# A complex-decay attention and expert kernel: the order of the program from a fixed table instead of a planner

## Chip, cores, metric

The kernel runs on 1 core of one Trainium2 chip. The metric is the device time of one execution in microseconds; before the change it is 220.39 us, the median of three runs (220.15 to 220.47).

## What is computed

Four batches, eight heads, 768 time steps, head width 48. Each step scales a 48x48 complex state per head by a decay and adds an outer product; the output row is read with `q` and goes through a layer norm and a two-layer network with 1536 hidden columns.

```python
scale = np.minimum(mag, 0.999) / (mag + 1e-06)        # mag = |a|
for t in range(S):
    new_re = ar * S_re - ai * S_im
    new_im = ar * S_im + ai * S_re
    S_re, S_im = (new_re + kv, new_im)                # kv = outer(k_t, v_t)
    y[:, :, t] = np.einsum('bhd,bhde->bhe', q[:, :, t], S_re)
...
xn = (x - mu) / np.sqrt(var + 1e-06) * g_ln           # x: y with its heads side by side
out = x + np.maximum(xn @ w_ch1, 0.0) @ w_ch2
```

## The kernel before

The 768 steps of a batch are cut into chunks of 128, and two chunks make a pair: 12 pairs `P`, 24 chunks `n`. Lines are those of the profile.

**Decays and phases of a pair.** SP loads `are`, `aim` (128 x 768) and, chunk by chunk, `k`, `q` and `vf` (line 402 to 411). ScalarE takes the logarithm and the inverse of `are` (429, 431), VectorE forms the ratio `r` (423), its square `r2` is made by GpSimd, VectorE or ScalarE, ScalarE takes log(1 + r2) (444), VectorE puts the log magnitude `l` together and clamps it (449, 451). TensorE sums it over time with triangular matrices `u_e` (463, `dec`), ScalarE takes both exponentials `e` and `en` (468). For the phase ScalarE takes the arctangent `th` (472), TensorE sums it (479, 482, `ph`), VectorE keeps the last row as the carry `car` (492) and makes the absolute value `sh` (499, or ScalarE 497), ScalarE takes sine and cosine into `trig` (502, 505). Logarithms and trigonometry need different tables in ScalarE, loaded at line 676, once for a unit of two pairs.

**Attention of a pair.** `ke` and `qe` are `k` and `q` times the exponentials, `ks` and `qs` those times cosine and sine (line 423; `tt` gives all of these one line, told apart by tile). `ks` and `qs` of a chunk are transposed, by TensorE (534) with a copy (384, 382) or by a DMA transpose on SP (542), fixed for each pair by `CROSSBAR`. `am` is the score matrix (558), `atm` its masked copy (423 from `banks` and `mask`), `gm` adds the chunk to the state (571 puts the old state in with an identity product, 575 adds), `G` scales it by the chunk's decay `dec`, `y` is the output (593, 596), `x` its copy. The decays of the two chunks come per unit: TensorE sums `l` (690), ScalarE takes `et` (697), TensorE spreads it (705), VectorE copies `dec` (709).

**Network of a pair.** Norm statistics (606, 607), `rstd` on GpSimd (624, 626), transposes of `x` (614), the copy `xT` (617), the first product (638), `relu` on ScalarE (647), the second product (656), `ot` on VectorE (662), the store (667). The first weights are folded with the norm's weights once, in the head: 27 matmuls (371) and nine copies.

**The order.** Every step is an `Op` with costs; `Graph.order` walks time with guessed costs, keys and slacks per engine, picks for each engine the next step, chooses between alternatives such as GpSimd or VectorE for `ke`, and gives out the eight PSUM banks. Steps marked `lock` are planned so that VectorE and GpSimd don't run them at once. Each engine then executes its instructions in the order so found. The weights `w1b` and `w2b` are loaded by GpSimd (352, 354) behind its constants.

Of the kernel before, what the change touches and what calls it, by code (L numbers as in the profile page):

```python
# [43 lines left out]
BIAS = {"abs": 0.402, "r2": 0.226, "ke": -1.349, "qe": 1.158, "kT": 1.307, "qT": 0.801, "wc": -0.23, "x": 0.392}  # L44
CHUNK = 0.212
SLACK = {"PE": 0, "ACT": 0.051, "DVE": 0.16, "POOL": 0.598, "SP": 0.016}
LATENCY = 0.18
WARM = 22.0


class Op:
# [8 lines left out]
class Graph:  # L60


    def __init__(self, rings, n_banks=8):
        self.ops, self.rings = {}, rings
        self.n_banks = n_banks
        self.bank = {}

    def add(self, name, eng, cost, group, pos, emit, needs=(), uses=(), ps=None, alt=None, tail=0.0, c=0, lock=False):
        assert name not in self.ops, name
        alts = {eng: (cost, tail)}  # L70
        for e, c_ in alt or ():
            alts[e] = (c_, tail)
        self.ops[name] = Op(name, alts, group, pos, emit, list(needs), list(uses), ps)
        self.ops[name].c = c
        self.ops[name].lock = lock

    def order(self, keys):
        ops = self.ops
        for op in ops.values():
            op.key = op.pos + keys[op.group] + (CHUNK * op.c)  # L80
        touch, owner_ops = {}, {}
        for op in ops.values():
            for kind, idx in op.uses:
                touch.setdefault((kind, idx), []).append(op)
            if op.ps:
                owner_ops.setdefault(op.ps[0], []).append(op)
        for op in ops.values():
            preds = {ops[n].name for n in op.needs}
            for kind, idx in op.uses:
                for o in touch.get((kind, idx - self.rings[kind]), ()):  # L90
                    preds.add(o.name)
            preds.discard(op.name)
            op.preds = [ops[n] for n in preds]
            for p in op.preds:
                p.users.append(op)
            op.left = len(op.preds)
        free = {e: 0.0 for e in ("PE", "ACT", "DVE", "POOL", "SP")}
        dma_free = lock_free = 0.0
        bank_free = [0.0] * self.n_banks
        bank_used = [None] * self.n_banks  # L100
        owner_left = {o: len(v) for o, v in owner_ops.items()}
        owner_end = {}
        ready = {e: [] for e in free}
        for op in ops.values():
            if op.left == 0:
                for e in op.alts:
                    ready[e].append(op)
        done, queued = [], []

        def choose(n):  # L110
            best = None
            if n == 2:
                for i in range(0, self.n_banks, 2):
                    if bank_used[i] is None and bank_used[i + 1] is None:
                        t = max(bank_free[i], bank_free[i + 1])
                        if best is None or t < best[0]:
                            best = (t, i)
            else:
                for i in range(self.n_banks):
                    if bank_used[i] is None:  # L120
                        t = (bank_used[i ^ 1] is None, bank_free[i])
                        if best is None or t < best[0]:
                            best = (t, i)
                if best:
                    best = (best[0][1], best[1])
            return best

        total = len(ops)
        while len(done) < total:
            pick = None  # L130
            for e, cands in ready.items():
                ests = []
                for op in cands:
                    t = free[e]
                    for p in op.preds:
                        t = max(t, p.end + (LATENCY if p.eng != e else 0.0))
                    if op.ps and op.ps[0] not in self.bank:
                        b = choose(op.ps[1])
                        if b is None:
                            continue  # L140
                        t = max(t, b[0])
                    if e in ("POOL", "DVE") and op.lock:
                        t = max(t, lock_free)
                    if len(op.alts) > 1:
                        main = next(iter(op.alts))
                        end = t + op.alts[e][0] + (BIAS[op.group] if e != main else 0.0)
                        if any(max(free[x], t if x == "POOL" else 0.0) + op.alts[x][0]
                               + (BIAS[op.group] if x != main else 0.0) < end - 0.01
                               for x in op.alts if x != e):
                            continue  # L150
                    ests.append((t, op))
                if not ests:
                    continue
                t0 = min(x[0] for x in ests) + SLACK[e]
                t, op = min((x for x in ests if x[0] <= t0), key=lambda x: (x[1].key, x[0]))
                if pick is None or t < pick[0]:
                    pick = (t, op, e)
            assert pick is not None, [o.name for v in ready.values() for o in v]
            t, op, e = pick
            cost, tail = op.alts[e]  # L160
            if e == "PE" and t < WARM:
                cost *= 2
            op.eng = e
            if op.ps and op.ps[0] not in self.bank:
                i = choose(op.ps[1])[1]
                self.bank[op.ps[0]] = i
                for j in range(i, i + op.ps[1]):
                    bank_used[j] = op.ps[0]
            free[e] = t + cost
            if e in ("POOL", "DVE") and op.lock:  # L170
                lock_free = t + cost
            op.start, op.cost = t, cost
            op.end = t + cost
            if tail and e == "POOL":
                for o, at in queued:
                    if at > t:
                        o.end += tail
                dma_free = max(dma_free, t + cost) + tail
                op.end = t + cost + tail + 1.8
            elif tail:  # L180
                queued.append((op, max(dma_free, t + cost)))
                dma_free = max(dma_free, t + cost) + tail
                op.end = dma_free + 1.8
            if op.ps:
                o = op.ps[0]
                owner_left[o] -= 1
                owner_end[o] = max(owner_end.get(o, 0.0), op.end)
                if owner_left[o] == 0:
                    i = self.bank[o]
                    for j in range(i, i + op.ps[1]):  # L190
                        bank_used[j] = None
                        bank_free[j] = owner_end[o] + LATENCY
# [13 lines left out]
def kernel(  # L206
# [116 lines left out]
    def c_ident():  # L323
        make_identity(nc, ident)
# [423 lines left out]
```

## Time and profile before

| | before |
|---|---|
| median of 3 runs | 220.39 us (220.15 to 220.47) |
| profiled execution | 218.72 us |
| its span, first to last instruction | 217.0 us |
| TensorE busy | 181.4 us, 1874 matmuls |
| VectorE, ScalarE, GpSimd busy | 167.5, 152.5, 68.6 us |
| moved by DMA | 38.84 MB, 179 GB/s |

The span is what the trace shows; the execution's own time lies 1.7 us above it. Busy time is the union of an engine's instructions. Matmuls overlap in the trace, so what one costs is the distance from its start to the next start and not its duration. An idle engine costs nothing unless the chain that ends last runs through it.

### The profile page before, as it was taken

Reading aid. Unit: us, or ns where it says so; the run is one execution under the profiler, and the core shown is the slowest. Engines: PE = TensorE matmul, PEld = TensorE weight load, DVE = VectorE, ACT = ScalarE, POOL = GpSimd, SP = SyncE. Lnnn points to the kernel's source line nnn. Section 1 sums busy time; section 2 is a strip of 40 time slices with the busy share of each in tenths; the row PEclk is TensorE's granted clock in tenths of the full one; section 3 lists DMA queues with packets and bytes.
Section 4 is the critical chain, followed back from the end, with each engine's and each line's share of the span. In section 5 each row is a group of like instructions: output and inputs, shape, how many; then the busy total and the mean of one; then the engine's idle time right before and its main releaser. Section 6 shows DMA issues by size and latency. Waiting matters only on the chain.

```text
span 217.0 us, 4784 instructions
## 1 busy us (share of the span) xinstructions
PE 181.4 (84%) x1874; PEld 132.7 (61%) x1875; DVE 167.5 (77%) x294; ACT 152.5 (70%) x188; POOL 68.6 (32%) x106
## 2 busy tenths in 40 slices
PE   0027565789899999988999899999999999899993
PEld 0012244347699668776586686677856688677861
DVE  0663288999799998999998897789989899772122
ACT  4545468679799878699486998989997882525410
POOL 8980103055003355303790012920057201301000
PEclk9999999699999999999999999999999999999999
DMA  6999999999999999499999899988983178720212
GB/s 180 310 199 197 193 238 234 217 199 284 194 226 184 242 266 194 84 220 246 234 232 190 188 142 232 244 179 186 201 167 93 37 121 210 101 73 3 73 67 78
DMA packets 137350, 38.84 MB, mean 179 GB/s; under 512 B 132336, under 2 KB 136944, under 8 KB 137328
## 3 DMA queue, kind: packets, MB, share of 16 engines
q1 hardware_dynamic: 135376, 36.19, 77.4%
q0 software_dynamic: 1952, 2.36, 6.3%
q8 instruction: 14, 0.23, 0.4%
q14 instruction: 8, 0.07, 0.1%
HBM read 28.31 MB, written 4.72 MB: 152 GB/s over the span
## 4 chain that ended last, share of the span: by engine, by line
PE 41%; DVE 23%; ACT 23%; DMA 5%; issue 4%; SPq 1%; DVEq 0%; ACTq 0%
PE banks L656 13%; PE banks L638 9%; ACT h L647 4%; PE banks L463 3%; DVE l L449 3%; ACT trig L502 3%; DVE l L451 3%; PE banks L558 3%; ACT trig L505 2%; PE banks L482 2%; ACT are L431 2%; DVE r L423 2%; ACT L676 2%; DVE sh L499 2%; PE banks L371 2%
## 5 line engine op out<-in xcount | busy, mean ns | idle before, releaser
L638 PE MATMUL banks<-xT,w1b 128*128 128x256 bf16 x432 | 52.8, 272 | 0.5 <-ACT h L647 0.3
L656 PE MATMUL banks<-w2b,h 128*128 128x384 bf16 x288 | 52.3, 326 | 0.0
L638 PEld LDWEIGHTS <-w1b 128*128 128x128 bf16 x432 | 40.6, 98 | 6.0 <-issue 1.1
L647 ACT ACTIVATE h<-banks 128x1024 bf16<-128x1024 f32 x36 | 36.4, 1021 | 11.0 <-PE banks L638 10.8
L656 PEld LDWEIGHTS <-h 128*128 128x128 bf16 x288 | 26.9, 98 | 15.1
L423 POOL TENSOR_TENSOR qe<-q,e 128x384 bf16<-128x384 f32 x24 | 23.6, 1003 | 27.5 <-ACT e L468 18.5
L423 DVE TENSOR_TENSOR atm<-banks,mask 128x1024 bf16<-128x1024 f32 x24 | 28.6, 1215 | 1.3 <-PE banks L558 1.1
L662 DVE SCALAR_TENSOR_TENSOR ot<-banks,rstd,x 128x384 f32<-128x384 f32 x24 | 14.7, 611 | 16.6 <-PE banks L656 12.4
L463 PE MATMUL banks<-l,u_e 128*128 128x384 f16 x48 | 11.0, 357 | 16.7 <-DVE l L451 16.7
L624 POOL TENSOR_SCALAR rstd<-mv 128x2 f32<-128x2 f32 x12 | 4.3, 361 | 62.0 <-DVE mv L607 62.0
L468 ACT ACTIVATE e<-banks 128x768 bf16<-128x768 f32 x12 | 9.7, 810 | 14.8 <-PE banks L463 14.3
L463 PEld LDWEIGHTS <-u_e 128*128 128x128 f16 x48 | 4.6, 103 | 21.0 <-issue 15.6
L676 ACT ACT_TABLE_LOAD x12 | 15.4, 1283 | 1.0 <-PEq L732 0.8
L558 PE MATMUL banks<-qsT,ksT 96*128 96x128 bf16 x192 | 14.5, 224 | 0.9 <-DMA ksT<-ks 0.9
L449 DVE SCALAR_TENSOR_TENSOR l<-r,w 128x768 f16<-128x768 f16 x12 | 11.4, 951 | 4.5 <-ACT r L444 4.5
L423 DVE TENSOR_TENSOR r<-aim,are 128x768 f16<-128x768 f32 x12 | 11.8, 985 | 4.0 <-ACT are L431 3.7
L502 ACT ACTIVATE trig<-banks 128x768 bf16<-128x768 int16 x12 | 9.7, 811 | 7.1 <-PE banks L482 4.4
L423 DVE TENSOR_TENSOR qs<-qe,trig 128x768 bf16<-128x768 bf16 x24 | 14.6, 623 | 0.1
L414 POOL TENSOR_SCALAR v<-vf 128x768 bf16<-128x768 f32 x12 | 10.6, 889 | 12.3 <-DMA vf<-in_v_dram 12.3
L505 ACT ACTIVATE trig<-sh,quarter 128x768 bf16<-128x768 f16 x12 | 11.3, 942 | 4.1 <-DVE sh L499 4.0
L423 DVE TENSOR_TENSOR ks<-ke,trig 128x768 bf16<-128x768 bf16 x24 | 13.9, 603 | 0.0
L558 PEld LDWEIGHTS <-ksT 96*128 96x128 bf16 x192 | 12.0, 100 | 3.1 <-DMA ksT<-ks 1.2
(79 smaller groups left out, 354.1 us busy)
## 6 DMA issues: line engine op xcount, KB each, us to landing
are<-in_a_re_dram SPq DMA_DIRECT2D x12, 384.0 KB, 4.8
aim<-in_a_im_dram SPq DMA_DIRECT2D x12, 384.0 KB, 4.9
k<-in_k_dram SPq DMA_DIRECT2D x24, 192.0 KB, 4.0
q<-in_q_dram SPq DMA_DIRECT2D x24, 192.0 KB, 3.8
vf<-in_v_dram SPq DMA_DIRECT2D x24, 192.0 KB, 3.9
out_dram<-ot SPq DMA_DIRECT2D x24, 192.0 KB, 2.2
w1b<-in_moe_w_ch_dram POOLq DMA_DIRECT2D x1, 1152.0 KB, 9.7
w2b<-in_moe_w_ch_dram POOLq DMA_DIRECT2D x1, 1152.0 KB, 17.0
```

Of the source, the lines that this page charges most:

```text
L414: add(("v", P), "POOL", .82, lock=True, emit=lambda: nc.gpsimd.tensor_scalar(out=T("v", P), in0=T("vf", P), scalar1=1.0, scalar2=0.0, op0= ...
L423: engine(name).tensor_tensor(**kw)
L449: nc.vector.scalar_tensor_tensor(out=flat(T("l", P)), in0=flat(T("r2", P)), scalar=0.5, in1=flat(T("w", P)), op0=ALU.mult, op1=ALU.add)
L463: nc.tensor.matmul(heads(ps[:, c, 0:DM]), lhsT=u_e[:, c, j], rhs=step(T("l", P), j), start=(j == 0), stop=(j == R - 1))
L502: add(("sin", P), "ACT", .7, lambda: act(out=T("trig", P)[:, 1], in_=v16(), func=AF.Sin, scale=TWO_PI_SAFE / TURN), needs=[("ph", P)], use ...
L505: add(("cos", P), "ACT", .83, lambda: act(out=T("trig", P)[:, 0], in_=T("sh", P), func=AF.Sin, scale=-TWO_PI_SAFE / TURN, bias=quarter), n ...
L558: nc.tensor.matmul(ps[:, h], lhsT=T("ksT", n)[0:D2, h], rhs=T("qsT", n)[0:D2, h], start=True, stop=True)
L638: nc.tensor.matmul(ps[:, jj], lhsT=w1b[:, dc, ts(gi * JG + jj, C)], rhs=T("xT", P)[:, dc].rearrange("p c t -> p (c t)"), start=(dc == 0), ...
L647: add(("relu", P, gi), "ACT", .91, lambda gi=gi, o=o: act(out=T("h", P)[:, ts(gi, JG)], in_=bank2(o).rearrange("p s (j t) -> p (s j) t", t ...
L656: nc.tensor.matmul(bank(("o", n))[:, 0:DM], lhsT=T("h", P)[:, j, ts(c, C)], rhs=w2b[:, j], start=(j == 0), stop=(j == NJ - 1))
L662: add(("ot", n), "DVE", .54, lambda n=n, c=c: nc.vector.scalar_tensor_tensor(out=T("ot", n), in0=bank(("o", n))[:, 0:DM], scalar=T("rstd", ...
L676: nc.scalar.preload_act_table_set({"log": "natural_log_exp_and_others", "trig": "trig_and_small"}[name])
```

## The change

**Table.** `KEYS`, `BIAS`, `CROSSBAR` and the planner go. `PLAN` is one list of steps for all engines, each with its engine and, where it has one, its first PSUM bank; `Graph.run` asserts the dependences and emits the steps in that order. Which engine does a step, which transposes go over DMA and where the tables are loaded all stand in the list.

**Halves.** `PARTS = {0: 2}`: pair 0 runs its decay and phase steps in two halves of four heads, with one PSUM bank each.

**Decays.** They are taken for a whole pair: 16 one-column matmuls read the last row of `e` (line 547), and `G` is scaled only after a pair's second chunk; after the first it is a plain copy, and the second chunk adds to the same bank without the identity product. The 48 rows of cosine and of sine lie at partitions 0 and 64, so that `ks`, `qs`, their transposes and `G` use all 128.

**Weights.** `w1b` and `w2b` are issued after a one-column probe of a tile that the load of `k` (pair 0, second chunk) or `aim` (pair 1) writes.

**Fill-ins.** `warm` steps are matmuls of 256 columns on constants into a free bank; the table has 52, all ahead of the first transposes.

**Engines.** `r`, `ks` and `qs` may run on GpSimd, `relu` on VectorE, `G`, `xT`, `car` and `dec` on ScalarE; `ot` may be split into a scaling on ScalarE (`oa`) and a sum on GpSimd; `atm` may be masked on GpSimd.

```diff
-CROSSBAR = {"ks": (6, 7, 8, 9, 10, 11), "qs": (3, 4, 5, 6, 7, 8, 9, 10, 11)}
+PARTS = {0: 2}
+GATES = {"gate.0": "k.0.1", "gate.1": "aim.1.0"}
+PLAN = """
+ue:G car0.1:G are.0.0:S pad.ks.0:G car0.0:G tab.log.0:A ln.0.0:A iv.0.0:A ident:G cmat.0:G are.0.1:S one:G
...
-    for op in g.order(KEYS):
-        op.emit()
+    g.run(PLAN)
...
+        g.add(name, lambda: nc.gpsimd.tensor_copy(out=probe, in_=t()[:, 0, 0:1]), needs=[GATES[name]])
...
+                        nc.tensor.matmul(bank(f"dps.{P}")[ds(a * HALF, D), ds(h, 1)],
+                                         lhsT=T("e", P)[96:C, R - 1, ts(h, D)],
+                                         rhs=ident[96:C, C - 1:C], start=True, stop=True)
...
-                    if not nfirst:
-                        nc.tensor.matmul(ps, lhsT=ident[0:D2, 0:D2],
+                    if c == 0 and not nfirst:
+                        nc.tensor.matmul(ps, lhsT=ident,
...
-                                         lhsT=T("ks", P)[:, c, h, 0:D2],
+                        nc.tensor.matmul(heads(ps)[:, h], lhsT=T("ks", P)[:, c, h],
...
+                if c == 0:
+                    add(f"G.{n}", lambda n=n: put(f"G.{n}", T("G", n),
+                                                  heads(bank(f"gm.{P}")[:, 0:DM])),
...
+                if eng(f"relu.{P}.{gi}") == "ACT":
+                    act(out=dst, in_=src, func=AF.Relu)
+                else:
+                    nc.vector.tensor_scalar(out=dst, in0=src, scalar1=0.0, scalar2=None, op0=ALU.max)
...
+            add(f"oa.{n}", lambda n=n, c=c: nc.scalar.mul(
+                out=T("ot", n), in_=bank(f"o.{n}")[:, 0:DM], mul=T("rstd", P)[:, ds(c, 1)]),
...
+                if eng(f"ot.{n}") == "POOL":
+                    nc.gpsimd.tensor_tensor(out=T("ot", n), in0=T("ot", n), in1=T("x", n), op=ALU.add)
...
+        g.add(f"warm.{i}", lambda i=i: nc.tensor.matmul(
+            bank(f"warm.{i}")[:, 0:256], lhsT=u_e[:, 0, 0], rhs=u_e[:, 1].rearrange(
+                "p j t -> p (j t)"), start=True, stop=True), needs=["ue"], ps=(f"warm.{i}", 1))
```

The order is shown at three places (the number behind a name is its buffer). The first is SP at the program's start, before:

```order
L402 DMA are_64<-in_a_re_dram 128x8x96
L402 DMA aim_67<-in_a_im_dram 128x8x96
L402 DMA are_65<-in_a_re_dram 128x8x96
L402 DMA aim_68<-in_a_im_dram 128x8x96
L402 DMA are_66<-in_a_re_dram 128x8x96
L402 DMA aim_69<-in_a_im_dram 128x8x96
L407 DMA k_73<-in_k_dram 128x8x48
L407 DMA q_70<-in_q_dram 128x8x48
```

and now:

```order
L434 DMA are_64<-in_a_re_dram 128x4x96 x2
L434 DMA aim_67<-in_a_im_dram 128x4x96 x2
L434 DMA are_65<-in_a_re_dram 128x8x96
L434 DMA are_66<-in_a_re_dram 128x8x96
L434 DMA aim_68<-in_a_im_dram 128x8x96
L393 DMA k_73<-in_k_dram 128x8x48
L359 DMA gln<-in_moe_g_ln_dram 128x3x1
L393 DMA k_73<-in_k_dram 128x8x48
L393 DMA q_70<-in_q_dram 128x8x48
L434 DMA aim_69<-in_a_im_dram 128x8x96
L393 DMA q_70<-in_q_dram 128x8x48
```

The loads of pair 0 come in half tiles, its second `k` stands ahead of both `q`, and the last of `aim` between them.

The second is GpSimd where it issues the weights, before (the memsets fill the unused columns of `ks` and `qs`):

```order
L339 AFFINE_SELECT cmat<-cmat 128x384 x3
L294 MEMSET ks_112 128x16x32
L294 MEMSET ks_113 128x16x32
L294 MEMSET ks_114 128x16x32
L294 MEMSET qs_115 128x16x32
L294 MEMSET qs_116 128x16x32
L294 MEMSET qs_117 128x16x32
L352 DMA w1b<-in_moe_w_ch_dram 128x3x1536
L354 DMA w2b<-in_moe_w_ch_dram 128x12x384
L423 TENSOR_TENSOR qe_110<-q_70,e_99 128x384 x2
```

and now:

```order
L351 COPY probe<-k_73 128x1
L355 DMA w1b<-in_moe_w_ch_dram 128x3x1536
L345 MEMSET qs_113 128x32x16
...
L351 COPY probe<-aim_68 128x1
L403 TENSOR_SCALAR v_78<-vf_76 128x768
L345 MEMSET qs_114 128x32x16
L277 TENSOR_TENSOR qe_109<-q_71,e_98 128x384 x2
L357 DMA w2b<-in_moe_w_ch_dram 128x12x384
L277 TENSOR_TENSOR ke_107<-k_74,en_100 128x384 x2
```

The two weight loads no longer stand side by side: the second waits behind the `v` of pair 0 and the `qe` of pair 1.

The third is VectorE where the network of pair 0 begins, before:

```order
L423 TENSOR_TENSOR ks_112<-ke_109,trig_103 128x16x48
L423 TENSOR_TENSOR r_85<-aim_68,are_65 128x768
L384 COPY ksT_118<-banks 96x1024
L384 COPY ksT_119<-banks 96x1024
L606 BN_STATS stats_144<-x_134 128x6
L607 BN_AGGR mv_147<-stats_144 128x2
L423 TENSOR_TENSOR atm_127<-banks,mask 128x1024
L423 TENSOR_TENSOR atm_128<-banks,mask 128x1024
L423 TENSOR_TENSOR r_86<-aim_69,are_66 128x768
L449 SCALAR_TENSOR_TENSOR l_90<-r_87,w_82 128x768
L451 TENSOR_SCALAR l_90<-l_90 128x768
L662 SCALAR_TENSOR_TENSOR ot_162<-banks,rstd_152,x_133 128x384
```

and now:

```order
L277 TENSOR_TENSOR ks_111<-ke_107,trig_102 128x16x48 x2
L274 COPY qsT_123<-banks 128x1024
L274 COPY qsT_122<-banks 128x1024
L698 TENSOR_SCALAR h_158<-banks 128x1024
L274 COPY ksT_118<-banks 128x1024
L653 BN_STATS stats_141<-x_131 128x6
L654 BN_AGGR mv_145<-stats_141 128x2
L277 TENSOR_TENSOR qs_115<-qe_108,trig_103 128x16x48 x2
L277 TENSOR_TENSOR atm_126<-banks,mask 128x1024
L277 TENSOR_TENSOR atm_124<-banks,mask 128x1024
L698 TENSOR_SCALAR h_158<-banks 128x1024
```

Two of the pair's three relu (`h`, line 698) stand on VectorE, and the ratios `r` have left it.

## Rows read from the trace of the kernel before

**Rows 1.** The page: busy time, share and instructions of each engine
```profile
PE 181.4 (84%) x1874; PEld 132.7 (61%) x1875; DVE 167.5 (77%) x294; ACT 152.5 (70%) x188; POOL 68.6 (32%) x106
```

**Rows 2.** Stretches: length, busy of PE, PEld, DVE, ACT, POOL, clock, DMA
```profile
25.00:43.20 18.20, 11.14 (x66) 7.13 (x67) 15.45 (x25) 12.11 (x15) 2.63 (x3) 0.91 1.11 227
43.20:190.00 146.80, 139.55 (x1586) 105.91 (x1585) 134.80 (x244) 120.07 (x151) 50.19 (x62) 1.00 0.90 189
190.00:213.50 23.50, 23.48 (x200) 16.69 (x197) 7.33 (x14) 7.11 (x8) 0.92 (x2) 1.00 0.16 57
```

**Rows 3.** Chain that ended last: start us, length us, what
```profile
0.79 3.54 DMA are<-in_a_re_dram
...
11.86 1.45 PE banks L463 x4
...
43.33 0.65 PE banks L463 x4
43.98 0.88 PE banks L371 x4
...
82.92 0.45 PE banks L705 x8
...
201.75 3.93 PE banks L638 x36
205.68 7.82 PE banks L656 x48
```

**Rows 4.** Timeline of TensorE, 50 to 57 us: start us, duration us, what
```profile
50.38 0.18 PE L593 MATMUL banks<-v,atm 128*128 128x48 bf16 x1
50.41 0.18 PE L596 MATMUL banks<-G,qsT 96*128 96x48 bf16 x1
...
54.49 0.33 PE L571 MATMUL banks<-G,ident 96*96 96x384 bf16 x1
54.66 0.50 PE L575 MATMUL banks<-v,ks 128*96 128x48 bf16 x8
55.00 0.61 PE L558 MATMUL banks<-qsT,ksT 96*128 96x128 bf16 x8
55.44 0.33 PE L479 MATMUL banks<-car,pick 96*128 96x384 f16 x1
...
56.43 0.61 PE L534 MATMUL banks<-ident,ks 128*96 128x128 bf16 x8
```

**Rows 5.** Groups by line and shape: busy us, mean ns of one
```profile
L647 ACT ACTIVATE h<-banks 128x1024 bf16<-128x1024 f32 x36 | 36.4, 1021 | 11.0 <-PE banks L638 10.8
L423 DVE TENSOR_TENSOR atm<-banks,mask 128x1024 bf16<-128x1024 f32 x24 | 28.6, 1215 | 1.3 <-PE banks L558 1.1
L676 ACT ACT_TABLE_LOAD x12 | 15.4, 1283 | 1.0 <-PEq L732 0.8
L431 ACT ACTIVATE are<-w 128x768 f32<-128x768 f32 x12 | 10.1, 845 | 0.3
L382 ACT CAST x<-banks 128x384 bf16<-128x384 f32 x18 | 8.4, 479 | 6.9 <-PE banks L596 6.9
```

**Rows 6.** Landing of loads: of `q` before 60 us, and of `w1b`
```profile
DMA to landing us min/median/max: 3.4/3.9/13.4
w1b<-in_moe_w_ch_dram POOLq DMA_DIRECT2D x1, 1152.0 KB, 9.7
```

**Rows 7.** Line 451, `qe`: ns min/median/max; all of 451; GpSimd's timeline at 10 us
```profile
L451 DVE TENSOR_SCALAR l<-l x12: 359/361/1775, 10.0 to 162.2; 128x768 f16<-128x768 f16 x12
L423 POOL TENSOR_TENSOR qe<-q,e x24: 903/914/1616, 14.2 to 166.1; 128x384 bf16<-128x384 f32 x24
L451 DVE TENSOR_SCALAR l<-l 128x768 f16<-128x768 f16 x12 | 8.1, 675 | 0.4
...
10.13 1.46 POOL L294 MEMSET qs<- 128x512 bf16 x3
```

**Rows 8.** Waits of SP's queue: us in total, times, longest
```profile
SPq L667 <- DVE ot L662: 35.5, 11, 6.9
```

More of the change, by code (lines that the diff above doesn't have):

```diff
@@ new lines @@
+relu.0.0:A4 decc.1:A7 r.3.0:G gm.2:P6 qs.2.0.0:V mm1.0.2.1:P0 am.3:P4 iv.4.0:A G.2:A6 r2.3.0:A qs.2.0.1:V
+qT.5:P7 gm.3:P6 atm.2:V2 atm.3:V4 y.2:P2 mm2.1.0:P3 y.3:P4 mm2.0.0:P5 mm2.1.1:P3 relu.0.2:V0 u.3.0:A r.4.0:G
+rstd.0:G l.3.0:V x.2:A2 xtr.2:P2 mm2.0.1:P5 mm2.1.2:P3 x.3:V4 mm2.0.2:P5 k.4.0:S dec.3.0:P0 xtr.3:P4 k.3.1:S
+ke.2.0.1:V r2.4.0:A u.4.0:A tab.trig.1:A th.3.0:A G.3:V6 qsT.5:V7 xT.2:A2 ot.1:V3 xT.3:V4 are.6.0:S
+ke.2.0.0:G ks.2.0.1:G tab.log.2:A en.3.0:A0 ph.3.0:P6 e.3.0:A0 ot.0:V5 l.4.0:V ks.2.0.0:G mm1.1.0.0:P2
@@ L83, in order @@
             for kind, idx in op.uses:
-                touch.setdefault((kind, idx), []).append(op)
+                touch.setdefault((kind, idx), []).append(op.name)
             if op.ps:
-                owner_ops.setdefault(op.ps[0], []).append(op)
-        for op in ops.values():
-            preds = {ops[n].name for n in op.needs}
-            for kind, idx in op.uses:
[L90 to L183, printed above, removed]
-            if op.ps:
[L185 to L192, printed above, removed]
-            for x in op.alts:
-                ready[x].remove(op)
-            done.append(op)
-            for u in op.users:
-                u.left -= 1
-                if u.left == 0:
-                    for x in u.alts:
-                        ready[x].append(u)
@@ L201, in order @@
-        self.span = max(o.end for o in done)
-        return done
+                group.setdefault(op.ps[0], []).append(op.name)
+        done, holder = set(), {}
+        for op in steps:
+            for n in op.needs:
+                assert n in done or n not in planned, (op.name, n)
+            for kind, idx in op.uses:
+                for n in touch.get((kind, idx - self.rings[kind]), ()):
+                    assert n in done, (op.name, n)
+            if op.ps:
+                owner, n_banks = op.ps
+                for i in range(self.bank[owner], self.bank[owner] + n_banks):
+                    old = holder.get(i)
+                    assert old == owner or all(n in done for n in group.get(old, ())), (op.name, old)
+                    holder[i] = owner
+            op.emit()
+            done.add(op.name)
@@ L284 @@
     half_n = pool.tile([C, R], FP32, name="half_n")
+    probe = pool.tile([C, 1], FP32, name="probe")
     cmat = pool.tile([C, ND, DM], FP16, name="cmat")
@@ new lines @@
+    g.add("one", c_one)
+    g.add("ue", c_ue)
+    g.add("uth", c_uth, needs=["ue"])
+    g.add("pick", c_pick)
+    g.add("zdec", lambda: [nc.gpsimd.memset(t, 0.0) for t in tiles["dec"]])
+    g.add("ident", lambda: make_identity(nc, ident))
+    g.add("mask", c_mask)
+    for i in range(RINGS["car"]):
+        g.add(f"car0.{i}", lambda i=i: nc.gpsimd.memset(tiles["car"][i], WINDOW))
+    for dc in range(ND):
+        g.add(f"cmat.{dc}", lambda dc=dc: c_cmat(dc))
+    for nm in ("ks", "qs"):
+        for i in range(RINGS[nm]):
+            g.add(f"pad.{nm}.{i}", lambda t=tiles[nm][i]: nc.gpsimd.memset(
+                t.rearrange("p c h (a x) -> p (c h a) x", a=2)[:, :, D:HALF], 0.0))
@@ L396, in pair_ops @@
         last = pp == PB - 1
[L398 to L404 removed]
+        NS = PARTS.get(P, 1)
```

707 lines of the change are left out of this document (393 added, 314 removed), and 7 rows, old and new, of tables (KEYS, RINGS).

## The prediction

> **What bounds the kernel now.** I read the busy shares first [rows 1]: TensorE is busy 84% of the span, VectorE 77%, ScalarE 70%, GpSimd 32%. A share is an average over stages, so the next view is the busy time by stretch [rows 2]. From 43.2 us to 190 us TensorE is busy 139.55 of 146.8 us with VectorE close behind (134.80) and ScalarE at 120.07; from 190 to 213.5 TensorE is full (23.48 of 23.5) while VectorE and ScalarE do 7 us each. Up to 43.2 us nobody is full: from 25 to 43.2 TensorE shows 11.14 of 18.2. So there are three stages: a head of 43 us in which one chain runs, a body in which TensorE is nearly full, and a tail of pure expert matmuls. The chain of waits says the same [rows 3]: it starts with the load of the first `are` tile, and ends with 36 and 48 matmuls back to back.
>
> How much of the body is real work? Busy spans of matmuls overlap, so I price TensorE by the spacing of starts [rows 3, 4]. Lines 638 and 656 cost 12 x 3.93 and 6 x 7.82 us, together 94.1. A block of eight `am` matmuls or transposes takes 0.44 (55.00 to 55.44), a row of `y` matmuls 0.0256 each (50.38, 50.41), eight `gm` 0.34 (54.66 to 55.00), the identity product 0.17, four `dec` matmuls 0.65, one phase `ph` 0.98 (55.44 to 56.43), eight of line 705 0.45, one of line 371 0.22, one `xtr` block 0.17 (three of the 128-column kind). By count: am 10.6, y 9.0, gm 6.8, identity 2.7, dec 7.8, ph 11.8, sums of line 690 3.9 (at the four 384-column matmuls' 0.65), line 705 2.7, transposes 7.9, xtr 4.1, line 371 5.9. The sum is 167.3 us. Of this 9.4 is done by 43.3 us (two dec, two ph, one 690, one 705, four transpose blocks, two am, eleven of line 371); the other 157.9 takes the 170.2 us from 43.3 to 213.5, so TensorE works at 92.8% there.
>
> **The change part by part.**
>
> *Head, the largest term.* Now the first pair is done in two halves of four heads, and ScalarE's order for it is fixed. A 768-wide activation takes 0.84, one of half width about 0.48, a table load 1.28 [rows 5]. Up to the last cosine of pair 0 ScalarE does in the new order: 7 half steps of the log part (3.4), four full ones for pairs 1 and 2 (3.4), four half exponentials (1.9), one more log (0.84), the table (1.28), 2 half and 2 full arctangents (2.6), and 7 half steps of carry, absolute value, sine and cosine (3.4): 16.8 us. They start when half an `are` tile has landed. That landing isn't in the trace: the full tile takes 3.54 from 0.79 [rows 3], a transfer can't be quicker than half of that, and I take 2.8, nearer the full one. So ScalarE ends at 0.8 + 2.8 + 16.8 = 20.4 if it never waits, and it is the busiest engine there. VectorE's last three half products (0.3 each), eight transposes and two copies follow, and `am` of chunk 0 starts near 23. Bounds for the moment at which TensorE becomes dense: 23 if nothing waits, 30 if the query tile is late (next paragraph). I take 25, against 43.3 before.
>
> *First weights.* `w1b` is now issued after a probe of `k`, with the `q` tiles still behind on SP. The load of `w1b` took 9.7 us; a `q` load takes 3.9 in the median and 13.4 in the one case that ran beside the weights [rows 6]. Issued near 12, `w1b` lands near 23, in time for line 373. A `q` of pair 0 issued near 11.5 lands at 15.5 by the median, where its cover is the ScalarE chain to 20.4, or at 25 by the worst row, which pushes the dense start to 30. In before both weights were in flight, now one, so I stay nearer the median.
>
> *Fill-ins.* 52 matmuls of 256 columns on constants. At the head's pace (four 384-column matmuls in 1.45 at 11.86, against 0.65 at 43.33 [rows 3]) one costs 0.24: 23 before the first `dec` are 5.5 us, hidden behind ScalarE's log part up to 7.5, and 25 more fit between `dec` and the first phase at 15. Their price is nothing while ScalarE is the head's engine; without that cover it would be 52 x 0.24 = 12.5. What they may give is the pace: before, the first row at the quick pace is that of 43.33.
>
> *TensorE's work.* Removed: line 690, -3.9; 8 of 16 identity products, -1.4. The `ks` weights are 128 columns instead of 96, like those of `y`: if `gm` follows `y`'s 0.0256 per matmul it saves 20 x 0.135 = 2.7; if it stays, nothing. I take the saving, since `y`'s matmuls have the same 48 columns and the same weights' shape. Added: two transpose blocks, +0.9; the decays, 128 one-column matmuls instead of 48, between 0.0256 (y) and 0.056 (line 705) each, so 3.3 to 7.2 instead of 2.7; their weights have half of line 705's 96 columns, so I take a little over a third of the way up, +2. Sum -5.1: 162.2 us, bounds 160.8 to 167.4. The Trainium skill, page TensorE: Matmul & The Clock Gate, ties its fast weight load to 128 weights (section Weight-path perf modes) and prices any other load at columns over 1.2 in ns (section LDWEIGHTS); by it `gm` takes the saving and the decays are 128 x 40 ns, an estimate of 5.1, +2.4 instead of +2, which would end the sum at 199.4 instead of 199.0. No run here shows one-column matmuls with 48-column weights yet. At line 705's row the decays would end it at 201.7.
>
> *Other engines.* VectorE loses about 51 instructions (8 r, 7 absolute values, 9 ot, 9 G, 8 products, 10 xT) at its mean of 0.55 (134.80 over 244, [rows 2]), -28, and gains 16 relu. A relu from PSUM on VectorE isn't in the trace; the nearest row is `atm` at 1.215 with the same 1024 columns [rows 5], below it the 1.02 of ScalarE's; I take 1.215: +19.4. VectorE goes from 167.5 to about 159. ScalarE gives 16 relu (-16.3) and six `et` (-5), and takes four table loads, seven absolute values and some 33 short copies and scalings: about +11 + 16, net +5, to 158. GpSimd takes 8 r, 8 products, 16 ke less 8 qe and 9 sums; at 0.914 per 384 columns [rows 7] that is some +37, to 105. None passes TensorE's 162, so their edits cost nothing in the sum as long as TensorE is what ends last. All 24 masks stay on VectorE in the table, so the new branch that would put one on GpSimd costs and gives nothing.
>
> *The sum.* By 25 us TensorE has done 7.0 (dec of pairs 0 and 1, three ph, one decay, four transpose blocks, one am). The other 155.2 at the old 92.8% take 167.2 and end at 192.2; the last `ot` and its store add the old 3.5 (213.5 to 217.0). Span 195.7, against 217.0: -21.3. The profiled execution took 218.72 for its span of 217.0, so 197.4; the median of the runs, 220.39, lies 1.67 above the profiled one, which gives 199.
>
> **Rivals.**
>
> *VectorE and GpSimd in each other's way, 210 us.* The clamp of `l` (line 451) takes 0.36 in the median, 1.78 at 10.0 us, where GpSimd was filling tiles; a `qe` on GpSimd takes 0.91, 1.62 at worst [rows 7]. The old planner kept such pairs apart; the table has no such rule, and GpSimd goes to half of the span. VectorE has some 97 instructions of this kind. Half of them meeting a GpSimd instruction with half of its 1 us left adds 24 us; the clamps of before, 8.1 us in all against 12 x 0.36, show 3.8. I price it at 16, to 175. Less 13 done by 25 us and 7 behind the last mask, 155 at VectorE's old 92% (134.80 of 146.8) take 168.5; with 25 before and 13 for the last pair behind its mask (3.9 each for lines 685 and 706, 1.2 relu, 3 store, five short steps) the span is 206.5. The same working with 159 gives 189, under TensorE's 195.7; it decides from some 166 on. Against it: most of VectorE's long work reads PSUM. The Trainium skill's page SBUF — State Buffer, section Who interferes with whom, says that GpSimd shares a port pair with VectorE as an exclusive lock, held for the whole instruction; by it this rival is what moving work to GpSimd brings, and the clamp's longest row agrees.
>
> *The head is not shortened as it says, 205 us.* The `q` tiles land behind `w1b`, dense start at 30, and the fill-ins, which end before the transposes, leave 2 us at the slow pace: 199 + 5 + 1 or so. For it: 13.4 in rows 6.
>
> *Slower than before: loads behind stores and transposes on SP, 224 us.* The table puts loads just ahead of their use, with 28 transposes and 24 stores between them in one queue; the last pair's `k` loads stand behind the store of chunk 13. SP already waits 35.5 us for `ot`, up to 6.9 at once [rows 8], but before with few loads left behind it. If each of 12 pairs then waits 2.1 us beyond its cover (half of a load's 3.9), 25 us come on top. It passes 220 from 1.8 per pair. Against it: rings of three tiles, so that most loads are a pair ahead.
>
> **How the numbers follow.** Forecast 0.62, port rival 0.17, head rival 0.10, SP rival 0.11. Only the last, most of it, is slower. Low end: dense at 23, 96% instead of 92.8%: 23 + 162 + 3.5 + 3.4 = 192, with 1 for work at its bound. High end: the port rival and 3 more, 213; the SP rival and part of the tails are left out. A difference within 0.2%, the least that a measurement of this kernel can tell, is 0.02: only between the port rival's worst and the SP rival.
>
> **What would show it.** Line 373 (the `w1` products) starting at 23 to 26; line 685 and 706 blocks at the same 0.109 and 0.163 per matmul; TensorE near 95% busy from there; eight `gm` in about 0.2; VectorE's relu near 1.2. Wrong if VectorE shows over 170 us busy with clamps and products stretched (port), if line 373 starts after 29 (head), or if ScalarE and GpSimd wait on loads for over 10 us after 50 us (SP).

## Result and profile after

The median is 209.14 us (208.03 to 211.35, four executions) against 220.43 (220.15 to 220.76) of the kernel before: ratio 0.947 [0.942, 0.952]. Ratios, here and below, leave out the slow executions, which lie over some 1.5% above the fastest of the same kernel; medians and ranges have all of them. The change is faster and inside the range of 191 to 213, but the forecast of 199.0 promised 21 us and 11 came. The profiled execution took 208.62 us, its span is 206.8.

The page of the changed kernel, busy time and slices, answers to [rows 1]:

```profile
PE 176.3 (85%) x1999; PEld 132.6 (64%) x2001; DVE 168.0 (81%) x276; ACT 156.9 (76%) x219; POOL 106.7 (52%) x131
PE   5666930689998899989979997997999899999993
DVE  0679960299999899999999899799998997774752
PEclk9999995599999999999999997899999999999998
```

Three engines were forecast well (ScalarE 158, GpSimd 105, TensorE judged by spacing below), VectorE was not: 168.0 instead of 159. The slices show a hole in TensorE and in VectorE at the seventh and eighth place, 31 to 41 us, with TensorE's granted clock at half in the same two places. The stretches of the changed kernel, as in [rows 2] with the last one ending at 206.8 (columns: span, then busy time of PE, PEld, DVE, ACT, POOL with counts, granted clock, DMA share, GB/s):

```profile
25.00:43.20 18.20, 7.76 (x65) 4.24 (x64) 7.05 (x8) 7.31 (x12) 6.16 (x8) 0.72 1.06 234
43.20:190.00 146.80, 138.00 (x1661) 106.14 (x1659) 134.74 (x216) 125.36 (x170) 84.65 (x84) 0.99 0.96 187
190.00:206.80 16.80, 13.30 (x130) 9.59 (x128) 9.67 (x16) 2.77 (x5) 4.46 (x7) 0.97 0.23 83
```

From 25 to 43.2 us TensorE does 7.76 of 18.2; before it did 11.14 there. The head was to be over by 25. Its TensorE timeline shows that it was, and then stopped:

```profile
23.25 0.61 PE L590 MATMUL banks<-qsT,ksT 128*128 128x128 bf16 x8
23.77 2.75 PE L373 MATMUL banks<-w1b,gc 128*128 128x512 bf16 x11
26.85 0.81 PE L373 MATMUL banks<-w1b,gc 128*128 128x512 bf16 x3
38.04 0.48 PE L618 MATMUL banks<-v,ks 128*128 128x48 bf16 x8 [10.38 <-POOL v L403]
38.67 2.73 PE L373 MATMUL banks<-w1b,gc 128*128 128x512 bf16 x6
```

`am` of chunk 0 and line 373 start where the prediction put them (23 and 23 to 26). Then TensorE waits 10.38 us for `v` from GpSimd, and afterwards runs at half pace: six matmuls of line 373 take 2.73 us at 38.67, eleven took 2.75 at 23.77. GpSimd's timeline says why `v` was late:

```profile
11.77 0.18 POOL L351 COPY probe<-k 128x1 f32<-128x1 f32 x1 [4.33 <-DMA k<-in_k_dram]
11.90 1.01 POOL L355 DMA_DIRECT2D w1b<-in_moe_w_ch_dram  x1
...
37.01 0.18 POOL L351 COPY probe<-aim 128x1 f32<-128x1 f32 x1 [20.11 <-DMA aim<-in_a_im_dram]
37.16 0.83 POOL L403 TENSOR_SCALAR v<-vf 128x768 bf16<-128x768 f32 x1
...
38.43 1.78 POOL L277 TENSOR_TENSOR qe<-q,e 128x384 bf16<-128x384 f32 x2
40.16 1.09 POOL L357 DMA_DIRECT2D w2b<-in_moe_w_ch_dram  x1
```

The second probe stands 20.11 us in front of `v`, two `qe` and the second weights. `aim` of pair 1, which it is meant to wait for, had been read by VectorE at 10.2 us. But `RINGS` gives `aim` three tiles, so pair 4 writes the tile of pair 1, and in the table `aim.4.0:S` stands ahead of `gate.1:G`. The probe therefore waits for the load of pair 4, the second of the two issues in this row of SP's queue:

```profile
30.82 1.81 SPq L434 DMA_DIRECT2D aim<-in_a_im_dram  x2
```

Asked for that issue alone, the trace names the probe as what waited for it, and its landing, 5.2 us behind 31.8, is the moment at which the probe runs:

```profile
L434 SPq DMA_DIRECT2D aim<-in_a_im_dram x1: 877/877/877, 31.8 to 31.8; - x1
...
  POOL probe L351: 20.1, 1
...
DMA to landing us min/median/max: 5.2/5.2/5.2
```

The second thing is VectorE. Two of its lines in the changed kernel (minimum, median and longest in ns):

```profile
L455 DVE SCALAR_TENSOR_TENSOR l<-r,w x13: 544/951/1896, 7.8 to 160.6; 128x768 f16<-128x768 f16 x11, 128x384 f16<-128x384 f16 x2
L457 DVE TENSOR_SCALAR l<-l x13: 260/360/1679, 8.3 to 161.9; 128x768 f16<-128x768 f16 x11, 128x384 f16<-128x384 f16 x2
```

and one such place, on VectorE, then on GpSimd, then on TensorE:

```profile
121.43 1.67 DVE L455 SCALAR_TENSOR_TENSOR l<-r,w 128x768 f16<-128x768 f16 x1
123.14 1.68 DVE L457 TENSOR_SCALAR l<-l 128x768 f16<-128x768 f16 x1
124.74 0.68 DVE L274 COPY ksT<-banks 128x1024 bf16<-128x1024 bf16 x1
```

```profile
121.06 1.23 POOL L277 TENSOR_TENSOR ke<-k,en 128x384 bf16<-128x384 f32 x1
122.36 2.24 POOL L277 TENSOR_TENSOR ks<-ke,trig 128x768 bf16<-128x768 bf16 x1
```

```profile
125.47 0.37 PE L618 MATMUL banks<-v,ks 128*128 128x48 bf16 x8 [1.77 <-DVE ksT L274]
125.69 0.82 PE L685 MATMUL banks<-xT,w1b 128*128 128x256 bf16 x6
```

The clamp is over at 124.8, right after GpSimd's `ks` at 124.6: 1.68 us for an instruction of 0.36 in the median. TensorE waits 1.77 us for the copy behind it.

### The profile page after: what moved, and what is told of

Read it like the earlier page. It is cut to its first block, busy times and chain, and to the rows that moved or that the text cites. A ratio compares the mean times of both kernels' runs of the same rounds, so it can differ in the third digit from the quotient of the medians.

```text
span 206.8 us, 5060 instructions
## 1 busy us (share of the span) xinstructions
PE 176.3 (85%) x1999; PEld 132.6 (64%) x2001; DVE 168.0 (81%) x276; ACT 156.9 (76%) x219; POOL 106.7 (52%) x131
## 4 chain that ended last, share of the span: by engine, by line
PE 42%; DVE 31%; issue 18%; POOL 7%; ACT 1%; POOLq 0%; DVEq 0%
PE banks L706 14%; PE banks L685 13%; DVE l L455 5%; DVE atm L277 4%; PE banks L590 4%; DVE ks L277 3%; DVE h L698 3%; PE banks L483 2%; DVE qs L277 2%; DVE stats L653 2%; PE banks L465 2%; PE banks L640 2%; DVE x L274 1%; PE banks L567 1%; DVE ot L720 1%
## 5 line engine op out<-in xcount | busy, mean ns | idle before, releaser
L696 ACT ACTIVATE h<-banks 128x1024 bf16<-128x1024 f32 x20 | 20.4, 1022 | 11.1 <-PE banks L685 11.0
L277 DVE TENSOR_TENSOR qs<-qe,trig 128x768 bf16<-128x768 bf16 (+1 forms) x23 | 13.5, 606 | 11.4 <-POOL qe L277 11.1
L698 DVE TENSOR_SCALAR h<-banks 128x1024 bf16<-128x1024 f32 x16 | 19.3, 1212 | 2.8 <-PE banks L685 2.8
L277 POOL TENSOR_TENSOR ke<-k,en 128x384 bf16<-128x384 f32 x16 | 16.5, 1042 | 5.6 <-ACT en L469 2.9
L277 POOL TENSOR_TENSOR r<-aim,are 128x768 f16<-128x768 f32 x8 | 14.9, 1859 | 8.2 <-ACT are L439 7.6
L618 PE MATMUL banks<-v,ks 128*128 128x48 bf16 x160 | 7.5, 186 | 12.2 <-POOL v L403 10.4
L455 DVE SCALAR_TENSOR_TENSOR l<-r,w 128x768 f16<-128x768 f16 (+1 forms) x13 | 14.7, 1135 | 1.0 <-ACT r L451 1.0
L590 PE MATMUL banks<-qsT,ksT 128*128 128x128 bf16 x192 | 15.0, 223 | 0.3 <-DVE h L698 0.2
L277 DVE TENSOR_TENSOR ks<-ke,trig 128x768 bf16<-128x768 bf16 (+1 forms) x21 | 13.8, 680 | 0.2
L590 PEld LDWEIGHTS <-ksT 128*128 128x128 bf16 x192 | 12.4, 99 | 1.9 <-issue 0.5
L653 DVE BATCH_NORM_STATS2 stats<-x 128x6 f32<-128x384 bf16 x24 | 13.1, 548 | 0.1
## 6 DMA issues: line engine op xcount, KB each, us to landing
w1b<-in_moe_w_ch_dram POOLq DMA_DIRECT2D x1, 1152.0 KB, 10.5
w2b<-in_moe_w_ch_dram POOLq DMA_DIRECT2D x1, 1152.0 KB, 12.5
```

What stands on the lines that cost most here:

```text
L277: {"DVE": nc.vector, "POOL": nc.gpsimd}[eng(name)].tensor_tensor(**kw)
L455: nc.vector.scalar_tensor_tensor(out=S_("l"), in0=S_("r2"), scalar=0.5, in1=S_("w"), op0=ALU.mult, op1=ALU.add)
L590: nc.tensor.matmul(ps[:, h], lhsT=T("ksT", n)[:, h], rhs=T("qsT", n)[:, h], start=True, stop=True)
L618: nc.tensor.matmul(heads(ps)[:, h], lhsT=T("ks", P)[:, c, h], rhs=T("v", P)[:, c, h], start=nfirst, stop=True, skip_group_check=True)
L653: nc.vector.bn_stats(out=T("stats", n), in_=T("x", n))
L696: act(out=dst, in_=src, func=AF.Relu)
```

## Experiments

Two theories for the missing 10 us: the probe behind a reused buffer, and VectorE and GpSimd holding each other up. A third stood against both: the loads are late by themselves. Kernels with a shorter table have other line numbers (e1 to e4 up to eight lower, e5 seven higher). Ratios are to the kernel before on the same chip; e1 to e4, e5 to e8, e9 to e11 and e12 ran on four different chips, so kernels of two groups are compared by ratio. Most kernels scatter by 2 to 5 us, four by 7 to 11 (e6, e9, e10, e11), and ratios whose intervals overlap are not told apart.

**e1: a tile of its own for the probe.**

```diff
-"aim": 3,
+"aim": 4,
```

> One number changes: the ring of `aim` tiles goes from three to four, so the load of pair 4 no longer writes the tile of pair 1 that GpSimd's second probe reads. The order of every engine stays. Theory (the probe stood 20 us behind a later load into its own buffer, and the hole of TensorE from 28 to 38 us is that wait): the probe runs at about 17 us, `v` of pair 0 right behind it, TensorE goes on after 28 us, and the 10 us come back: 198 to 201 us. Rival 1 (the hole is a lack of loads: with the second weights going out some 15 us sooner, the `q`, `k` and `are` tiles come late and TensorE waits elsewhere before 50 us): 204 to 209. Rival 2 (the probe waits for something else): it stays at 37 us and the time at 209.

204.9 us (202.35 to 205.44), ratio 0.929 [0.921, 0.938]. GpSimd's timeline of e1, then VectorE's:

```profile
16.98 0.53 POOL L348 COPY probe<-aim 128x1 f32<-128x1 f32 x1
24.14 0.83 POOL L400 TENSOR_SCALAR v<-vf 128x768 bf16<-128x768 f32 x1 [6.63 <-DMA vf<-in_v_dram]
```

```profile
21.01 1.02 DVE L274 TENSOR_TENSOR qe<-q,e 128x384 bf16<-128x384 f32 x2 [3.15 <-DMA q<-in_q_dram]
```

The probe runs at 16.98 and the hole is gone: from 25 to 43.2 TensorE does 17.45 of 18.2 us. So the shared tile was the cause of the hole. Only 4 of the 10 us came back, though, and the time lies in the band of rival 1, late loads. This profile shows one: a `q` of pair 0, issued at 11.17, a microsecond ahead of `w1b`, took 9.7 us to land (the prediction's head rival; the 11.2 us that the texts below name belong to a later `q`, issued beside `w2b`).

```profile
DMA to landing us min/median/max: 9.7/9.7/9.7
```

Line 373 started at 29.1. With that as the dense start the prediction's own sum gives a span of 199.8 (29.1 + 167.2 + 3.5), and this profile's is 200.5; the other three executions, 2 to 3 us longer, have no profile.

**e2: both weights close together.** e1 with `wl.1:G` moved right behind `gate.1:G`.

> As the kernel with four `aim` tiles, and the load of `w2b` goes out right behind its probe, at about 17 us, while `w1b` (issued at 11.9) is still in flight. If the gates matter because two weight loads beside the tile loads starve the first ones: `w1b` lands 3 to 6 us later, line 373 starts at 27 to 30 instead of 24, and the time is 3 to 5 us over that of four tiles alone. If the 16 DMA engines have room there: within 1 us of it.

203.3 us, 0.927 [0.920, 0.934], not told apart from e1. `w1b` was not delayed (10.6 us to land, line 373 at 23.4); the tile loads paid: `v` of pair 0 waited 12.9 us for `vf`, to 30.95. At the end the time does not tell `w2b` issued at 17 us from `w2b` issued at 33, as in e1.

**e3: no fill-ins.** e1 without the 52 `warm` steps.

> As the kernel with four `aim` tiles, without the 52 fill-in matmuls. Theory that they only keep the granted clock up: the phases, transposes and `w1` products of the head run at the lower level for some 3 to 8 us, and the time is 1 to 3 us over that of four tiles alone. Rival, that they are free but bring nothing: within 0.5 us of it. If they delay the real matmuls of the head instead: 0.5 to 2 us below it.

201.4 us (199.2 to 204.1), 0.911 [0.902, 0.919]: 4% better than the changed kernel, and lower than e1. My theory of a loss fell, and the gain is more than any of the three cases allowed. The pace without fill-ins, TensorE's timeline of e3, and with them, of the changed kernel:

```profile
15.18 1.44 PE L457 MATMUL banks<-l,u_e 128*128 128x384 f16 x4 [0.71 <-DVE l L449]
```

```profile
15.09 0.81 PE L465 MATMUL banks<-l,u_e 128*128 128x384 f16 x4 [0.39 <-DVE l L457]
```

They do quicken the head's matmuls, but that pace is hidden behind ScalarE. Why e3 beats e1 stays open: in its profile the `q` landed in time (line 373 at 24.8), and its granted clock was 1.00 in two executions, where e1's four lay between 0.958 and 0.971.

**e4 and e8: the first pair whole**, with and without fill-ins, in place of `PARTS = {0: 2}`.

```diff
-PARTS = {0: 2}
+PARTS = {}
```

> As the kernel with four `aim` tiles, with the first pair done whole again: each merged step stands where its later half stood, all else in the same order. Theory that the halves make the head short: the first logarithm waits for a full `are` tile (3.5 us instead of about 2.7), and no step of the second half runs beside one of the first, so line 373 starts at 27 to 30 us instead of 24 and the time is 3 to 6 us over that of four tiles alone. Rival, that the fixed order of ScalarE did it and the halves hardly anything: line 373 within 1.5 us and the time within 1 us.

> Four `aim` tiles, no fill-ins, first pair done whole. With fill-ins the whole first pair gave 201.4 us against 204.9 for halves, though its line 373 started at 27.7 and not at 24. If that is real (the halves cost TensorE, ScalarE and VectorE more short instructions than the earlier start is worth): 197 to 200 us here. If the two gains are one and the same (a kernel without fill-ins or with fewer of them in the way of the first pair): 200.5 to 202.5. If the halves do make the head short once the fill-ins are gone: 203 to 206.

201.4 us, 0.918 [0.909, 0.927], and 201.6 us, 0.917 [0.911, 0.922]. Line 373 starts at 27.7 and 26.8: the halves do save 2 to 3 us of head, but neither e4 nor e8 is told apart from e3. So the halves bring nothing that can be measured at the end, nor do fill-ins cost anything with a whole pair.

**e5: a quiet GpSimd.** e3, and from pair 4 on GpSimd's products and its casts of `v` touch only a few columns, so this kernel leaves out most of that work.

```diff
-{"DVE": nc.vector, "POOL": nc.gpsimd}[eng(name)].tensor_tensor(**kw)
+{"DVE": nc.vector, "POOL": nc.gpsimd}[eng(name)].tensor_tensor(**few(name, kw))
```

> Four `aim` tiles, no fill-ins, and from pair 4 on GpSimd's products (`ke`, `qe`, `ks`, `qs`, `r`) and its casts of `v` cover only a few columns of each tile (the rest of the tile keeps old values, so this kernel leaves out most of that work). VectorE keeps all its instructions. Port theory (VectorE and GpSimd hold each other up, which is what took VectorE from the forecast 159 us to 169.6): the clamps of line 457 come back to 0.36 us and the sums of line 455 to 0.95, VectorE's busy time falls by 8 to 12 us to 158 to 161, and the time falls to 190 to 195 us from 201.4 without fill-ins. Rival (the long instructions are stretched by the traffic of the DMA engines or by PSUM): they stay, VectorE at 167 or more. Second rival (TensorE, not VectorE, ends the body, so that the collisions cost nothing): VectorE falls, the time stays above 198.

194.2 us, 0.884 [0.879, 0.888], against 0.911 for e3: some 6 us. From 80 to 160 us, the stretches of e5:

```profile
80.00:120.00 40.00, 39.43 (x458) 30.62 (x457) 37.45 (x65) 39.01 (x54) 8.43 (x24) 1.00 1.01 213
120.00:160.00 40.00, 39.24 (x480) 29.38 (x479) 34.79 (x67) 35.50 (x49) 10.55 (x25) 1.00 1.12 214
```

and of e3:

```profile
80.00:120.00 40.00, 34.23 (x393) 26.13 (x391) 38.95 (x55) 34.47 (x47) 25.60 (x23) 1.00 0.95 202
120.00:160.00 40.00, 37.47 (x464) 28.44 (x462) 38.25 (x65) 34.87 (x48) 21.95 (x22) 1.00 1.00 198
```

With GpSimd at work VectorE is full (38.95 of 40) and TensorE starves at 34.23; with GpSimd quiet TensorE is full at 39.4. In the whole program the same 276 VectorE instructions take 156.7 instead of 169.6 us. The pages of e3 and e5:

```profile
PE 167.5 (84%) x1949; PEld 126.2 (63%) x1949; DVE 169.6 (85%) x276; ACT 156.2 (79%) x219; POOL 106.0 (53%) x131
PE 169.0 (88%) x1949; PEld 128.1 (66%) x1949; DVE 156.7 (81%) x276; ACT 156.0 (81%) x219; POOL 61.8 (32%) x131
```

The sums and clamps of `l` that start from 80 to 160 us, two rows of e3, then two of e5 (minimum, median and longest in ns):

```profile
L447 DVE SCALAR_TENSOR_TENSOR l<-r,w x7: 943/949/1665, 80.0 to 152.6; 128x768 f16<-128x768 f16 x7
L449 DVE TENSOR_SCALAR l<-l x7: 359/361/1674, 80.9 to 154.0; 128x768 f16<-128x768 f16 x7
L462 DVE SCALAR_TENSOR_TENSOR l<-r,w x7: 948/951/958, 81.6 to 147.5; 128x768 f16<-128x768 f16 x7
L464 DVE TENSOR_SCALAR l<-l x7: 359/359/361, 82.6 to 148.4; 128x768 f16<-128x768 f16 x7
```

The port theory holds: with GpSimd quiet none of them is stretched any more, while the DMA engines move as much as before (213 and 214 GB/s against 202 and 198), so the rival that blames their traffic falls, and with 194.2 us so does the one by which the collisions cost nothing. GpSimd's work is worth 6 us of the time, although e5's profile began line 373 at 30.2, 5 us later than e3's. Part of the 6 may be that GpSimd's results are ready sooner; that was not separated.

**e6 and e7: the first gate.** e3 with the probe on `q` of chunk 0 instead of `k`; e3 with `w1b` as GpSimd's first load, no probe.

> Four `aim` tiles, no fill-ins, and the first probe reads the query tile of chunk 0 instead of the key tile of chunk 1, so that `w1b` goes out when `q` of pair 0 has landed. With the gate on `k`, this `q` took 3.6 us in some profiles and 11.2 in the one with four tiles alone. Theory (`q` beside `w1b` is a matter of luck that costs up to 3 us of the head): `q` lands within 5 us, `w1b` is issued at about 15 and lands at 25 to 26, line 373 starts at 25 to 27, and the time is 1 us below to 1 us above the kernel without fill-ins, with less scatter. Rival (the later `w1b` ends the head): line 373 after 27.5 and the time 1.5 to 3 us over it.

> Four `aim` tiles, no fill-ins, and `w1b` goes out as GpSimd's first instruction with no probe ahead of it, as in the kernel before; `w2b` stays behind its probe. If the gate is a large part of what shortened the head: the `are`, `aim`, `k` and `q` tiles of pair 0 each land 2 to 5 us later, line 373 starts at 30 to 34 instead of 25, and the time is 5 to 9 us over the 201.4 of the kernel without fill-ins. If the fixed order of the program alone did it: line 373 within 2 us of 25 and the time within 1.5 us.

e6: 203.8 us (201.1 to 208.1), 0.922 [0.915, 0.928]; line 373 at 27.0, no less scatter: not better. The `q` landed in 3.4 and 4.3 us, as hoped, but `w1b` only at 26.9, and line 373 waited for it. e7: 205.3 us, 0.936 [0.931, 0.940]; line 373 at 31.0. ScalarE's timeline of e7 shows it waiting for VectorE's ratio, whose two half tiles of `aim` took 7.1 and 10.5 us to land beside `w1b`, 3.5 and 4.1 in e3:

```profile
9.71 0.52 ACT L447 ACTIVATE r<-r 128x384 f16<-128x384 f16 x1 [4.10 <-DVE r L277]
```

So the first gate is worth 6 us of head and some 5 at the end (0.936 against 0.911); holding `w2b` back longer brought nothing that can be measured (e2), and its probe, on a tile that is written again, cost 4 us (e1).

**e9 to e12: towards a better version.** e9: in the table of e3 `q.0.0:S` goes ahead of `aim.2.0:S`, and `gln:S` behind it. On e9, e10 gives GpSimd's eight `ks` and `qs` to VectorE, e11 gives `relu.3.1`, `4.0`, `5.1` and `7.0` to ScalarE, and e12 puts `q.2.1:S` ahead of `are.3.0:S` and `k.2.0`, `k.2.1` ahead of `are.4.0`, `aim.4.0`.

> Four `aim` tiles, no fill-ins, and on SP the second query tile of pair 0 goes ahead of `gln` and of the 384 KB `aim` tile of pair 2 (that is issued two places later). Theory (a `q` that is issued only 1 us ahead of `w1b` can fall behind it, and then line 373 starts at 29 to 30 as in the kernel with four tiles alone and in the one with a quiet GpSimd, not at 25): with 2 us more of a start it never does, line 373 starts at 24 to 26, and the median is 0.5 to 2 us below the 201.4 of the kernel without fill-ins. Rival (the start of the dense work no longer counts, since VectorE fills the body): within 0.5 us of it.

> As the kernel with the early query, and the eight rotations of `ks` and `qs` that the table gives to GpSimd (1.8 to 2.2 us each there) go to VectorE (about 0.6 each). Port theory by the rate of the quiet kernel (12.9 us of VectorE's time for 44 us less of GpSimd's, 0.29 per us): VectorE takes on 4.8 us and is spared 8 x 1.85 x 0.29 = 4.3, and TensorE's stops behind the longest locks go; VectorE's busy time stays at 168 to 171 and the time within 1 us, or 1 to 2 us lower if these eight cause more than their share. Rival (VectorE is just full of work, without a price for what GpSimd does): busy 173 to 175 and the time 3 to 5 us higher.

> As the kernel with the early query, and four of VectorE's sixteen relu (of the blocks 3, 4, 5 and 7) go to ScalarE. If VectorE ends the body between 80 and 160 us (it is busy there for 97% and ScalarE for 83 to 90%): VectorE 4.8 us less, ScalarE 4.1 more, the time 1.5 to 4 us lower. If ScalarE's chain is as tight as VectorE's: within 1 us. If ScalarE becomes the bound: 1 to 3 us higher.

> As the kernel with the early query (four `aim` tiles, no fill-ins), and on SP the second query tile of pair 2 goes ahead of the 384 KB tiles of pairs 3 and 4, and the two key tiles of pair 2 ahead of the `are` and `aim` tiles of pair 4. Theory (the executions at 206 to 211 us of the kernels with the early query and without fill-ins are those in which the query of pair 2, issued 1 us behind `w2b`, landed 12 us later, with GpSimd's products of all later pairs queued behind it): that tile goes out 5 to 8 us ahead of `w2b`, GpSimd and VectorE don't wait for it, no execution is over 204 us, and the median is 199 to 201.5. Rival (the two weight loads slow whatever load is beside them, and the next tile in line takes the same wait): executions of 205 to 211 remain, median 202 to 207.

e9: 206.2 us (200.4 to 211.0), 0.915 [0.909, 0.922]. e10: 203.2 (202.0 to 211.0), 0.920 [0.916, 0.925]. e11: 207.0 (201.9 to 210.1), with no ratio. e12: 204.9 (202.1 to 205.9), 0.928 [0.923, 0.933]. None beats e3, as e9 and e12 were to. In the four profiles line 373 starts in time, at 25.5, 24.8, 24.3 and 24.6. But in the profiled executions of e9 and e10 (208.2 and 210.9 us) TensorE stops for 6 to 7 us between 42 and 51 instead, with half the clock behind it. GpSimd's timeline of e9:

```profile
30.69 1.09 POOL L357 DMA_DIRECT2D w2b<-in_moe_w_ch_dram  x1
...
44.04 0.91 POOL L277 TENSOR_TENSOR qe<-q,e 128x384 bf16<-128x384 f32 x1 [9.37 <-ACT h L696]
```

The row blames ScalarE, which had long been done. Behind it is the `q` of pair 2, issued at 31.84, whose landing took 12.0 us, the longest of the `q` loads there; e10's row for the same wait names that load. In e11's profile (201.9 us) the same `q` landed in 5.9 us, and TensorE has no such stop; that this load decides whether an execution of the three takes 200 or 210 us is argued from these three profiles. e12 sent this tile ahead, and the next in line took the wait, on ScalarE:

```profile
45.58 0.84 ACT L437 ACTIVATE w<-are 128x768 f32<-128x768 f32 x1 [7.64 <-DMA are<-in_a_re_dram]
```

The rival stated for e12 holds in its profile (205.9 us): the needed tile that stands beside a weight load is late, by landings of 9.7 us in e1, 12.0 in e9, 11.7 in e10 and 11.6 here. The changed kernel escaped this by accident: its blocked probe held `w2b` back to 40 us.

e10 fits the price of the port, by one profile. Its page stands below that of e9, whose profile has the same late load:

```profile
PE 169.6 (82%) x1947; PEld 127.5 (62%) x1949; DVE 173.1 (84%) x276; ACT 156.8 (76%) x219; POOL 106.6 (52%) x131
PE 172.8 (83%) x1947; PEld 128.7 (62%) x1949; DVE 173.7 (83%) x284; ACT 157.2 (75%) x219; POOL 91.7 (44%) x123
```

Eight more instructions of about 0.6 us cost VectorE 0.6 us net: what left GpSimd gave back nearly all that VectorE took on. The 173 to 175 of the theory of mere work counted from e3's 169.6 and are no sign for it.

e11 took four relu, 4.8 us of work, off VectorE, and its two lowest times (201.9 and 203.7 us) show no gain over those of e9 (200.4 and 202.5). From 80 to 160 us its VectorE is busy for 70.6 of 80 us, ScalarE for 71.9, TensorE for 69.7. So none of the three is full there; that ScalarE's chain is as tight as VectorE's fits, but it was not followed.

## Why the prediction was right in sign and 10 us off

*Head.* Right up to 27.7 us: ScalarE's chain, `w1b` (issued 11.90, landed in 10.5), `am` at 23.25, line 373 at 23.77. The failed step is the moment at which TensorE becomes dense, "I take 25, against 43.3 before". In *First weights* I costed what is queued behind `w1b` and never what is queued behind the second probe, nor asked which load last wrote its tile. TensorE was dense from some 42 us instead, and e1 shows the cause and its price, 4 us of the 10.

*Fill-ins at nothing*: borne out at the end by e8 against e4 (0.917 and 0.918); e3 against e1 (0.911 and 0.929) is another 4 us and leaves it open. That the halves make the head short was right by 2 to 3 us at line 373 and worth nothing at the end.

*TensorE's work.* Eight `gm` cost 0.22 (125.47 to 125.69) against 0.34: 2.4 saved, 2.7 forecast. The decays were over-priced: TensorE's timeline of the changed kernel has

```profile
13.90 0.36 PE L547 MATMUL banks<-ident,e 32*48 32x1 bf16 x16 [1.59 <-ACT e L469]
```

16 in 0.36 us, at most 0.0225 each or 2.9 in all, where I took 4.7. The Trainium skill (TensorE: Matmul & The Clock Gate, section LDWEIGHTS) would make 40 ns of each load of 48 columns, an estimate of 5.1 us; the measurement decides against it as a spacing. Of the 95% busy that I named, the changed kernel shows 94% from 43.2 to 190 us, e3 92% there, and e5 98% from 80 to 160 us.

*Other engines.* relu on VectorE took 1.212 us as forecast. The other failed step is "None passes TensorE's 162, so their edits cost nothing in the sum as long as TensorE is what ends last": VectorE took 168.0, past the 166 from which my port rival decides. Where the head came as forecast, in e3 (line 373 at 24.8), the span is 198.9 against my 195.7, 3 us beyond the sum, which by that one profile is what this step cost it; all of GpSimd's hindrance is worth 6 (e5). The rival's own working (189 of span at 159, 206.5 at 175) gives 200.6 at e3's 169.6, and e3 shows 198.9, e1 200.5. So with the hole closed the mechanism of the rival that I gave 0.17 is what holds, at 12.9 us of VectorE's time where I had 16. That the time came out beside its 210 is chance, for 4 us of that were the probe's wait. e11 forbids saying that VectorE's busy time alone ends the kernel. The Trainium skill (SBUF — State Buffer, section Who interferes with whom) says the two engines share a port pair as an exclusive lock held for the whole instruction; the clamp of 1.68 us that ends with GpSimd's `ks` agrees, and so do the clamps of e5.

*SP rival*: GpSimd waits 3.4 us on `vf` and 2.7 on `k` after 50 us, and 6.9 on all loads together, under the 10 named. Its relative, loads beside `w2b`, showed only once the hole was closed.

## What to carry to other kernels

When a wait on a tile is used as a gate, ask which load wrote that tile last in program order, and what stands behind the waiting instruction on its engine. When work moves to GpSimd, add to VectorE's sum a price per microsecond of GpSimd: here 12.9 us for 44 us, some 0.3. Put a large load where no tile in flight beside it is needed before it has landed (9 to 14 us for these weights in e1 to e12), for freeing one wait on it brings up the next.

## What the runs showed of the hardware that I had not expected

The granted clock's row reads 1.00 at the start of every profile, while the four matmuls at 15.18 in e3 run at half pace; only falls that come later are seen in it. After TensorE stood still from 27.7 us the changed kernel's row shows 1.00 up to 31, 0.60 from 31 to 34 and 0.50 from 34 to 40, that is 1.2 of 2.4 GHz, and it is back at 1.00 from 42: the stop cost its own 10.4 us and then some 4 us of work at half pace. Tile loads beside the weights landed only when the weights did: in e3 `w2b`, issued at 30.05, took 13.2 us, and the loads issued at 30.99, 31.85, 33.55 and 39.19 took 12.5, 12.6, 11.7 and 6.8, so all landed from 43.4 to 46.0; only the one issued at 30.27 came sooner, after 6.9. VectorE and GpSimd take turns: at 121 us `l` (0.95 alone) ends 0.8 after GpSimd's `ke`, `ks` ends only 1.5 after `l`, and the clamp 0.2 after `ks`, so that each instruction pays for the other's.
